# Load order and planner margins, a seven-product first layer for part of two chunks, and v casts and q features moved to other engines, in a fused linear attention and MLP kernel

## The chip, the cores and the metric

The kernel runs on one core of one Trainium2 chip. The metric is device time of one execution in microseconds (us). The kernel before takes 297.5 us (median of 4 runs, 297.03 to 297.73). All the ratios below use runs that were labelled fast; a median is over all runs of a kernel. TensorE, VectorE, ScalarE, GpSimd and the queue of SyncE are called PE, DVE, ACT, POOL and SP in the profile's lines; PEld is PE's weight load, which overlaps its matmuls.

## The reference, cut to what matters

```python
# q, k, v: (batch 8, heads 8, seq 576, head_dim 64), float32
phi(x) = concat(relu(x) * cos(theta * pos), relu(x) * sin(theta * pos))   # 64 -> 128 features
kv  = phi(k)^T v ;  z = sum(phi(k))                  # per batch and head
x   = (phi(q) @ kv) / (phi(q) @ z + 1e-6)            # 4608 tokens x 512
h   = x @ w_in                                       # first layer, 512 -> 2048
out = (h * cos(h)) @ w_out                           # second layer, 2048 -> 512
```

The 4608 tokens are worked in 9 chunks of 512. Chunks 0 to 7 are the first 512 tokens of each of the 8 batches, roughly; chunk 8 collects the 64 left over of each.

## The kernel before: the parts that matter here

The kernel does not issue instructions in the order of the program text. It records steps (engine, cost, what they read and write) in a `Plan`; a small model of the engines and of two DMA rings then orders the steps of each engine. On the chip each engine takes its instructions strictly in that order. A step that the model thought ready, but that waits for a late DMA, holds up all that stands behind it on its engine.

```python
class Plan:
    SHARE, WAKE, LAND = {"HW": 0.42, "SW": 0.58}, {"HW": 1.1, "SW": 1.6}, 1.0   # the DMA model
    ...
    def run(self):            # up to 12 passes: forward with keys, backward for new keys
```

Loads of q, k and v go through SyncE; the weights through GpSimd. An order between the two is made by small GpSimd copies ("holds") which write one element of a tile after another load has landed:

```python
def hold_raw(nm):             # batch 1: first heads of k, q, v wait for the first quarter of w_out
    pl.add("POOL", 0.2, 0.3, 0, lambda: nc.gpsimd.tensor_copy(
        out=raw[nm][0:2, 0, 0, 0:1], in_=w_out_sb[0:2, 0, 0:1]),
        [("w_out", 0)], [((nm, 0), 0), ((nm, 0), 1)])

def attention(b):             # batches 2 to 7
    ...                       # loads of k, q, v
    for t in range(NT + 1):
        for g in range(2):    # cosine and sine half of the features
            prep(b, "k", t, g, "DVE" if g == 0 else "ACT", T + 1.2 * t)
    for t in range(NT + 1):
        cast_v(b, t, "DVE", T + 6 + 0.4 * t)            # v to float16
    kv(b, T + 8)
    for t in range(NT + 1):
        ...
        for g in range(2):
            prep(b, "q", t, g, "DVE" if g == 0 else "ACT", due)
    ...

def layer1(c):                # chunks 2 to 8: 16 tiles of 4 matmuls of 128x512
    for n in range(NJT):
        ...
        for cc in range(NCT):
            nc.tensor.matmul(M1[m], lhsT=w_in_sb[:, cc, j * P:(j + 1) * P], rhs=X[:, cc, :],
                             start=(cc == 0), stop=(cc == NCT - 1))
        gate(...)             # ACT: cos(h);  DVE: h * cos(h) -> gT
```

The second layer already uses seven products in place of eight (Strassen's scheme in Winograd's form) for all chunks but the first. In the profile's names, km, qm, vm are the raw loads, kp and qp the features, V the float16 v, qT the transposed q features, x and xT the attention's result and its transpose, gT the gated hidden layer, ch its cosine, S and T the sums of the seven products of the second layer, ost the output. M, TR and ATT are PSUM banks.

## Time and profile before

| stretch, us | what PE does | PE idle | VectorE busy | ScalarE busy |
|---|---|---|---|---|
| 20 to 40 | chunk 0, first layer | 1.6 | 13.6 of 20 | 14.1 |
| 40 to 62 | attention 1, chunk 0's second layer | 4.6 | 16.8 of 22 | 15.3 |
| 62 to 82 | chunk 1 | 0.35 | 18.9 of 20 | 18.8 |
| 82 to 228 | chunks 1 to 6, attention 2 to 7 | 1.3 | 135.8 of 146 | 95.5 |
| 228 to 275 | chunks 7 and 8 | 0 | 32.9 of 47 | 24.6 |

These are the lines of the windows view of the kernel before. For each stretch they give its length, then busy us and number of instructions of PE, its weight loads, VectorE, ScalarE and GpSimd, then the granted share of PE's clock, the DMA engines' busy share and GB/s:

```profile
20.00:40.00 20.00, 18.36 (x151) 14.86 (x149) 13.62 (x28) 14.14 (x23) 1.07 (x5) 0.86 1.06 259
40.00:62.00 22.00, 17.41 (x193) 11.52 (x191) 16.84 (x41) 15.34 (x26) 1.31 (x2) 1.00 0.94 251
62.00:82.00 20.00, 19.65 (x235) 16.23 (x233) 18.85 (x38) 18.75 (x33) 0.00 (x0) 1.00 1.05 254
82.00:228.00 146.00, 144.71 (x1306) 100.15 (x1305) 135.84 (x279) 95.51 (x152) 0.00 (x0) 1.00 0.85 195
228.00:275.00 47.00, 47.00 (x315) 30.65 (x314) 32.88 (x53) 24.57 (x37) 0.00 (x0) 1.00 0.10 38
```

From 62 us on PE is the bound. VectorE is close behind it in the middle: 135.84 of 146 us is 93%. Before 62 us PE waits for data. The timeline of SyncE's queue shows why (start us, us, what):

```profile
14.77 0.60 SPq L295 DMA_DIRECT2D vm<-in_v_dram  x1
15.48 0.60 SPq L298 DMA_DIRECT2D vm<-in_v_dram  x1
29.23 0.60 SPq L298 DMA_DIRECT2D km<-in_k_dram  x1
```

The hold covers only the first heads of v. The second half of batch 1's v is issued at 14.77 us, and k of batch 1, which is needed first, at 29.23. On ScalarE a cast of this early v then stands in front of other work, and near 53 us a feature of k of batch 2 stands in front of a qT copy on VectorE. In these timeline lines of ScalarE and VectorE the bracket tells how long the engine was idle before the line and what ended it:

```profile
24.41 0.73 ACT L329 ACTIVATE V<-vm 128x256 f16<-128x256 f32 x2 [3.17 <-DMA vm<-in_v_dram]
...
53.15 0.88 DVE L319 TENSOR_SCALAR kp<-km,CS 128x512 f16<-128x512 f32 x2 [1.98 <-DMA km<-in_k_dram]
53.95 0.68 DVE L378 COPY qT<-M 128x1024 f16<-128x1024 f16 x1
```

PE pays for it. These are its longest waits in 40 to 62 us (who waited for whom: us in total, times, longest):

```profile
PE M L444 <- DVE qT L378: 2.3, 1, 2.3
PE ATT L404 <- DVE qT L378: 0.8, 1, 0.8
PE M L444 <- DVE x L424: 0.7, 1, 0.7
```

In 82 to 228 us the waits view lists one wait of PE, for a copy on ScalarE:

```profile
PE M L613 <- ACT ost L624: 1.3, 2, 1.1
```

Last, the groups by shape in 82 to 228 us, for the durations of VectorE's work (busy us, mean ns of one; then its idle time before them):

```profile
L466 DVE TENSOR_TENSOR gT<-M,ch 128x512 f16<-128x512 f32 x82 | 54.5, 683 | 6.6 <-ACT ch L464 6.0
L595 DVE TENSOR_TENSOR S<-gT 128x1024 f16<-128x1024 f16 x23 | 15.4, 683 | 0.1
L332 DVE CAST V<-vm 128x512 f16<-128x512 f32 x25 | 9.1, 421 | 0.0
L319 DVE TENSOR_SCALAR kp<-km,CS 128x512 f16<-128x512 f32 x20 | 9.0, 476 | 0.0
```

### The profile page before, as it was taken

How to read it: one execution, taken by the hardware profiler on the slowest of the kernel's cores; microseconds unless marked ns; L12 is line 12 of the kernel's file. 1: busy time of each engine (PE TensorE's matmuls, PEld its weight loads, DVE VectorE, ACT ScalarE, POOL GpSimd, SP SyncE). 2: the span in 40 equal slices, each digit the busy share in tenths (PEclk: the TensorE clock that was granted, in tenths of full speed). 3: DMA queues.
4: the chain of work that ended last, by engine and by line, in shares of the span. 5: the costliest groups of instructions: out<-in, count | busy, mean ns of one | idle time of the engine just before them, and what ended most of it. 6: DMA issues, size and time to landing. Idle time of an engine off the chain costs nothing.

```text
span 295.5 us, 6280 instructions
## 1 busy us (share of the span) xinstructions
PE 276.6 (94%) x2460; PEld 194.4 (66%) x2460; DVE 239.3 (81%) x486; ACT 183.6 (62%) x293; POOL 8.9 (3%) x20
## 2 busy tenths in 40 slices
PE   6768998699999999999999999999999999999994
PEld 2446866268977677666766766676668566666783
DVE  2975786798999899988998999999879858665741
ACT  2945895698987756767386849575544554645320
POOL 1520020000000000000000000000000000000000
PEclk9977999999999999999999999999999999999999
DMA  6999979999956999999999939971925100300304
GB/s 214 322 228 213 289 189 257 310 337 191 273 162 157 182 234 250 230 210 297 215 233 298 265 101 241 231 188 46 143 59 170 41 0 2 142 2 1 123 21 142
DMA packets 77565, 53.27 MB, mean 180 GB/s; under 512 B 46048, under 2 KB 75232, under 8 KB 77536
## 3 DMA queue, kind: packets, MB, share of 16 engines
q1 hardware_dynamic: 72592, 48.12, 63.9%
q0 software_dynamic: 4224, 4.19, 8.7%
q10 hardware_dynamic: 720, 0.57, 0.6%
q8 instruction: 19, 0.31, 0.4%
q14 instruction: 10, 0.08, 0.1%
HBM read 36.74 MB, written 9.44 MB: 156 GB/s over the span
## 4 chain that ended last, share of the span: by engine, by line
PE 67%; DMA 15%; DVE 9%; ACT 5%; issue 2%; SPq 0%; ACTq 0%; DVEq 0%
PE M L613 28%; PE M L509 27%; DMA vm<-in_v_dram 7%; PE M L491 6%; DMA qm<-in_q_dram 6%; DVE gT L466 3%; DMA km<-in_k_dram 3%; PE ATT L404 2%; PE ATT L343 2%; ACT ch L464 2%; DVE x L424 1%; PE M L553 1%; ACT kp L316 1%; ACT qp L316 1%; DVE V L332 1%
## 5 line engine op out<-in xcount | busy, mean ns | idle before, releaser
L464 ACT ACTIVATE ch<-M,PIH 128x512 f32<-128x512 f32 x144 | 97.9, 686 | 60.4 <-PE M L509 57.0
L466 DVE TENSOR_TENSOR gT<-M,ch 128x512 f16<-128x512 f32 x144 | 96.8, 685 | 25.8 <-ACT ch L464 24.9
L509 PE MATMUL M<-xT,w_in_sb 128*128 128x512 f16 x384 | 93.8, 379 | 0.0
L613 PEld LDWEIGHTS <-gT 128*128 128x128 f16 x640 | 62.4, 98 | 18.4 <-issue 1.7
L509 PEld LDWEIGHTS <-w_in_sb 128*128 128x128 f16 x448 | 42.1, 98 | 35.0
L613 PE MATMUL M<-w_out_sb,gT 128*128 128x256 f16 x384 | 46.8, 273 | 1.3 <-ACT ost L624 1.3
L491 PE MATMUL M<-xT,w_in_sb 128*128 128x256 f16 x256 | 31.8, 282 | 1.6 <-ACT xT L448 1.6
L613 PE MATMUL M<-T,S 128*128 128x256 f16 x256 | 32.5, 273 | 0.0
L613 PE MATMUL M<-T,gT 128*128 128x256 f16 x256 | 32.2, 273 | 0.0
L613 PEld LDWEIGHTS <-S 128*128 128x128 f16 x256 | 25.1, 98 | 8.0
L491 PEld LDWEIGHTS <-w_in_sb 128*128 128x128 f16 x256 | 25.5, 101 | 5.9 <-issue 2.1
L316 ACT ACTIVATE qp<-qm,CS 128x512 f16<-128x512 f32 x38 | 25.3, 713 | 6.5 <-DMA qm<-in_q_dram 6.5
L316 ACT ACTIVATE kp<-km,CS 128x512 f16<-128x512 f32 x39 | 26.4, 713 | 1.4 <-DMA km<-in_k_dram 1.4
L424 DVE TENSOR_TENSOR x<-ATT,rec 128x512 f16<-128x512 f32 x33 | 22.8, 691 | 1.1
L319 DVE TENSOR_SCALAR qp<-qm,CS 128x512 f16<-128x512 f32 x42 | 18.7, 484 | 5.7 <-DMA qm<-in_q_dram 5.7
L595 DVE TENSOR_TENSOR S<-gT 128x1024 f16<-128x1024 f16 x32 | 21.6, 685 | 0.2
L319 DVE TENSOR_SCALAR kp<-km,CS 128x512 f16<-128x512 f32 x41 | 18.3, 487 | 2.4 <-DMA km<-in_k_dram 2.4
L404 PEld LDWEIGHTS <-qT 128*128 128x128 f16 x320 | 14.7, 98 | 6.3 <-issue 2.7
L404 PE MATMUL ATT<-kvz,qT 128*128 128x65 f16 x296 | 14.8, 194 | 1.6 <-DVE qT L378 0.8
L509 PE MATMUL M<-xR,w_in_sb 128*128 128x512 f16 x64 | 16.1, 379 | 0.0
L332 DVE CAST V<-vm 128x512 f16<-128x512 f32 (+1 forms) x42 | 13.7, 382 | 2.9 <-DMA vm<-in_v_dram 2.9
L343 PEld LDWEIGHTS <-kp 128*128 128x128 f16 x320 | 10.9, 97 | 2.8 <-ACT V L329 1.1
(66 smaller groups left out, 180.2 us busy)
## 6 DMA issues: line engine op xcount, KB each, us to landing
out_dram<-ost SPq DMA_DIRECT2D x33, 256.0 KB, 3.0
qm<-in_q_dram SPq DMA_DIRECT2D x8, 640.0 KB, 6.4
km<-in_k_dram SPq DMA_DIRECT2D x8, 640.0 KB, 5.9
qm<-in_q_dram SPq DMA_DIRECT2D x8, 512.0 KB, 7.0
km<-in_k_dram SPq DMA_DIRECT2D x8, 512.0 KB, 6.7
vm<-in_v_dram SPq DMA_DIRECT2D x6, 640.0 KB, 5.5
vm<-in_v_dram SPq DMA_DIRECT2D x6, 512.0 KB, 5.5
w_in_sb<-in_moe_w_in_dram POOLq DMA_DIRECT2D x4, 512.0 KB, 10.1
```

Of the source, the lines that this page charges most:

```text
L316: act(0.12 + 0.5 * f, due, lambda: nc.scalar.activation(out=out_, in_=in_, func=AF.Relu, scale=sc), rd, wr)
L319: dve(0.09 + 0.33 * f, due, lambda: nc.vector.tensor_scalar(out=out_, in0=in_, scalar1=0.0, scalar2=sc, op0=ALU.max, op1=ALU.mult), rd, wr)
L332: dve(0.09 + 0.33 * f, due, lambda: nc.vector.tensor_copy(out=out_, in_=in_), rd, wr)
L343: nc.tensor.matmul(bank[hb][:, hh * D1:(hh + 1) * D1], lhsT=kp[:, t, h].rearrange("p g d -> p (g d)"), rhs=V1[:, t, h, :], start=(t == 0), ...
L404: nc.tensor.matmul(bank[hb][:, hh * D1:(hh + 1) * D1], lhsT=a[:, h, :], rhs=z[:, h, :], start=(i == 0), stop=(i == len(parts) - 1))
L424: nc.vector.tensor_tensor(out=split(x16[n][:, hs, :], k), in0=A[:, :, :, 0:D], in1=split(rec[n][:, hs], k).unsqueeze(3).broadcast_to((P, k ...
L464: act(0.59, due, lambda: nc.scalar.activation(out=ch[c], in_=bank, func=AF.Sin, bias=PIH, scale=1.0), [key, "PIH"], [("ch", c)])
L466: dve(0.61, due, lambda: nc.vector.tensor_tensor(out=dst, in0=bank if len(dst.shape) == 2 else bank.rearrange("p (j s) -> p j s", j=dst.sh ...
L491: nc.tensor.matmul(M1[m][:, jj * 2 * P:(jj + 1) * 2 * P], lhsT=w_in_sb[:, cc, j * P:(j + 1) * P], rhs=X[:, cc, ts], start=(cc == 0), stop= ...
L509: nc.tensor.matmul(M1[m], lhsT=w_in_sb[:, cc, j * P:(j + 1) * P], rhs=X[:, cc, :], start=(cc == 0), stop=(cc == NCT - 1))
L595: dve(0.07 + 1.07 / NG, due, lambda: nc.vector.tensor_tensor(out=out_[:, sl], in0=a[:, sl], in1=b[:, sl], op=op), rd, wr)
L613: nc.tensor.matmul(M2[bank][:, tt * MH:(tt + 1) * MH], lhsT=a[:, j, tt * P:(tt + 1) * P], rhs=b[:, j, :], start=(first and tt == 0 and j = ...
```

## The change

There are three parts.

- **Loads.** All of v is held, the holds wait for the third quarter of w_in in place of the first of w_out, the loads of the first two batches keep a fixed order, and the planner's DMA model gets new rates and lands each later load 1 us later.
- **Seven.** The first layer of chunk 7 (three groups of four) and of chunk 8 (two groups) uses seven products of half size in place of eight. This needs sums of w_in, built in the memory of kp and qp after batch 7, differences of x, and adds of the products.
- **Moves.** The v casts of batches 2 to 7 go from VectorE to GpSimd; the half of their q features that VectorE made goes to ScalarE.

```diff
-    SHARE, WAKE, LAND = {"HW": 0.42, "SW": 0.58}, {"HW": 1.1, "SW": 1.6}, 1.0
+    SHARE, WAKE, LAND = {"HW": 0.40, "SW": 0.56}, {"HW": 1.1, "SW": 1.3}, 1.0
+    BUSY, MARGIN = 2.2, 1.0
...
-                        done[n] = now + self.LAND
+                        done[n] = now + self.LAND + (self.MARGIN if now > 13.0 else 0.0)
...                                        # "lane": a fixed order for the first two batches' loads
+    GATE1 = (w_in_sb[0:2, 0, Dff // 2 + 1:Dff // 2 + 2], [("w_in", 2)])
...
     def hold_raw(nm):
-        pl.add("POOL", 0.2, 0.3, 0, lambda: nc.gpsimd.tensor_copy(
-            out=raw[nm][0:2, 0, 0, 0:1], in_=w_out_sb[0:2, 0, 0:1]),
-            [("w_out", 0)], [((nm, 0), 0), ((nm, 0), 1)])
+        for h in (0, HB) if nm == ORDER1[2] else (0,):
+            pl.add("POOL", 0.2, 0.3, 0, lambda h=h: nc.gpsimd.tensor_copy(
+                out=raw[nm][0:2, h, 0, 0:1], in_=GATE1[0]),
+                GATE1[1], [((nm, h), 0), ((nm, h), 1)])
...
+    FAST1 = {B - 1: 3, B: 2}
...                                        # w_in_sums(): 8 sums of 128x1024 on VectorE
+        def tt(n, a, b, op, rd, wr):
+            for f in range(2):
+                fs = slice(f * JH * P // 2, (f + 1) * JH * P // 2)
+                dve(0.61, due, lambda fs=fs: nc.vector.tensor_tensor(
+                    out=WS[n][:, :, fs], in0=a[:, :, fs], in1=b[:, :, fs], op=op),
+                    wk + [(x, f) for x in rd], wr + [("WS%d" % n, f)])
...                                        # layer1_fast(): 7 products of 4 matmuls of 128x256 a group
+            d = product(A, -11, b11, xk, True, False)
+            copy(Y, A, zk[0], d)
+            d = product(Bk, -12, b21, xk, True, True)
+            plus(Y, Bk, zk[0], d)
+            out(Y, zk[0], 0, 0, d)
...                                        # five more products
         for t in range(NT + 1):
-            cast_v(b, t, "DVE", T + 6 + 0.4 * t)
+            cast_v(b, t, "POOL", T + 6 + 0.4 * t)
...
             for g in range(2):
-                prep(b, "q", t, g, "DVE" if g == 0 else "ACT", due)
+                prep(b, "q", t, g, "ACT", due)
```

More of the change, by code (lines that the diff above doesn't have):

```diff
@@ L36, in __init__, with add @@
         self.steps = []
-        self.wr, self.rd = {}, {}
-    def add(self, eng, occ, lat, due, fn, rd=(), wr=(), dma=None):
+        self.wr, self.rd, self.lanes = {}, {}, {}
+    def add(self, eng, occ, lat, due, fn, rd=(), wr=(), dma=None, lane=None):
         n = len(self.steps)
+        prev = self.lanes.get(lane)
+        if lane is not None:
+            self.lanes[lane] = n
         deps = set()
@@ L55, in add @@
         self.steps.append(dict(eng=eng, occ=occ, lat=lat, due=due, fn=fn,
-                               deps=deps, dma=dma, n=n))
+                               deps=deps, dma=dma, n=n, prev=prev))
         return n
@@ L85, in forward @@
                 users[d].append(s["n"])
+        follow = {s["prev"]: s["n"] for s in st if s["prev"] is not None}
+        left = [k + (s["prev"] is not None) for k, s in zip(left, st)]
         avail, start, done = [0.0] * len(st), [0.0] * len(st), [0.0] * len(st)
@@ L123, in forward @@
                         n = rings[r].pop(0)[2]
-                        done[n] = now + self.LAND
+                        if r == "SW" and not rings["SW"]:
+                            for x in rings["HW"]:
+                                x[0] = min(x[0], max(now, x[3]))
+                        done[n] = now + self.LAND + (self.MARGIN if now > 13.0 else 0.0)
                         release(n)
@@ L134, in forward @@
             free[e] = t + s["occ"]
+            if n in follow:
+                u = follow[n]
+                avail[u] = max(avail[u], t)
+                left[u] -= 1
+                if not left[u]:
+                    ready[st[u]["eng"]].append(u)
             if s["dma"] is None:
@@ L140, in forward @@
                 r = "SW" if e == "POOL" else "HW"
-                rings[r].append([free[e] + self.WAKE[r], s["dma"][0] / s["dma"][1], n])
+                wake = free[e] + self.WAKE[r]
+                late = wake + (self.BUSY if r == "HW" and rings["SW"] and not rings["HW"] else 0.0)
+                rings[r].append([late, s["dma"][0] / s["dma"][1], n, wake])
         return start, done
@@ L149, in backward @@
                 left[d] += 1
+            if s["prev"] is not None:
+                left[s["prev"]] += 1
         limit = [end - done[n] + start[n] for n in range(len(st))]
@@ L171, in backward @@
                 limit[d] = min(limit[d], late[n] - self.link(d, n) - (done[d] - start[d]))
+                left[d] -= 1
+                if not left[d]:
+                    ready[st[d]["eng"]].append(d)
+            d = st[n]["prev"]
+            if d is not None:
+                limit[d] = min(limit[d], late[n] - 0.01)
                 left[d] -= 1
@@ L265 @@
     Q_PE, X_PE = (), range(1, 3)
+    ORDER0, ORDER1, HOLDW = "qkv", "kqv", 1
+    GATE1 = (w_in_sb[0:2, 0, Dff // 2 + 1:Dff // 2 + 2], [("w_in", 2)])
     src = {"k": k, "v": v, "q": q}
@@ L299, in load @@
             nb = len(part) * R * D * 4 / 1e3
-            pl.add("SP", 0.65, 0, due, go4, (), [(x, 1 - n) for x in part], dma=(nb * NT, 355.0))
-            pl.add("SP", 0.65, 0, due, go5, (), [(x, n) for x in part], dma=(nb * (NT + 1), 355.0))
+            pl.add("SP", 0.65, 0, due, go4, (), [(x, 1 - n) for x in part], dma=(nb * NT, 355.0),
+                   lane="first" if b < 2 else None)
+            pl.add("SP", 0.65, 0, due, go5, (), [(x, n) for x in part], dma=(nb * (NT + 1), 355.0),
+                   lane="first" if b < 2 else None)
     def hk(nm, hs=range(H)):
@@ L330, in cast_v @@
                 out=out_, in_=in_, func=AF.Copy), rd, wr)
+        elif eng == "POOL":
+            pl.add("POOL", 0.9, 1.0, due, lambda: nc.gpsimd.tensor_copy(
+                out=out_, in_=in_), rd, wr)
         else:
@@ L500, in layer1 @@
             return
-        for n in range(NJT):
-            j = n // 2 + (n % 2) * JH if c < B else n
+        if c in FAST1:
+            layer1_fast(c, X, xk)
+        for n in range(4 * FAST1.get(c, 0), NJT):
+            j = n // 2 + (n % 2) * JH if c < B or c in FAST1 else n
             m = m1n[0] % NM1
@@ L512, in layer1, with flat, wsum @@
             gate(M1[m], ("M1", m), G[:, j, :], [("g", c % 2, j, t) for t in range(NT)], due + 1.5)
+    FAST1 = {B - 1: 3, B: 2}
+    CH2 = NCT // 2
+    def flat(t, dt=F16):
+        v = t.rearrange("p a b c -> p (a b c)") if len(t.shape) == 4 else t.rearrange(
+            "p a b c d -> p (a b c d)")
+        return v if dt == F32 else v.bitcast(F16)
+    kf, qf = flat(kp), flat(qp)
+    n2 = CH2 * JH * P
+    def wsum(ap, n):
+        return ap[:, n * n2:(n + 1) * n2].rearrange("p (c f) -> p c f", c=CH2)
@@ new lines, with w_in_sums @@
+    WS = {2: wsum(kf, 0), 3: wsum(kf, 1), 1: wsum(qf, 0), 4: wsum(qf, 1)}
+    Z3 = [[flat(raw[nm], F32)[:, i * SM:(i + 1) * SM] for i in range(3)] for nm in "kqv"]
+    XSS = [[flat(raw[nm])[:, 6 * SM + i * SM:6 * SM + (i + 1) * SM].rearrange(
+        "p (c s) -> p c s", c=CH2) for i in range(4)] for nm in "kq"]
+    def w_in_sums():
+        lo, hi = slice(0, JH * P), slice(JH * P, Dff)
+        W = w_in_sb
+        a11, a12, a21, a22 = W[:, 0:CH2, lo], W[:, CH2:, lo], W[:, 0:CH2, hi], W[:, CH2:, hi]
+        gone = {nm: [(nm + "p", t, g, h) for t in range(NT + 1) for g in range(2) for h in range(H)]
+                for nm in "kq"}
+        wk = [("w_in", g) for g in range(4)]
+        due = start[B - 1] - 6
+        def tt(n, a, b, op, rd, wr):
[4 more added lines that the diff above has]
+                    wk + [(x, f) for x in rd], wr + [("WS%d" % n, f)])
+        tt(3, a11, a21, ALU.subtract, [], gone["k"])
+        tt(1, a21, a22, ALU.add, [], gone["q"])
+        tt(2, WS[1], a11, ALU.subtract, ["WS1"], [])
+        tt(4, a12, WS[2], ALU.subtract, ["WS2"], [])
@@ new lines, with layer1_fast, tt, lhs @@
+    g1n = [0]
+    def layer1_fast(c, X, xk):
+        G = gT[c % 2]
+        tl, th = slice(0, TH), slice(TH, SM)
+        b11, b12 = X[:, 0:CH2, tl], X[:, 0:CH2, th]
+        b21, b22 = X[:, CH2:, tl], X[:, CH2:, th]
+        w0, ww = start[c], width[c]
+        XS = XSS[c % 2]
+        def tt(n, a, b, rd, wr=()):
+            dve(0.33, w0 - 1 + 0.3 * n, lambda: nc.vector.tensor_tensor(
+                out=XS[n], in0=a, in1=b, op=ALU.subtract), xk + rd, [("XS", c % 2, n)] + list(wr))
+        tt(0, b12, b11, [], (hk("k") + hk("q") + hk("v") + ["AL"]) if c == B - 1 else ())
+        tt(2, b22, b12, ["AL"])
+        tt(1, b22, XS[0], [("XS", c % 2, 0)])
+        tt(3, b21, XS[1], [("XS", c % 2, 1)])
+        ng = JH // 2
+        for g in range(FAST1[c]):
+            A, Bk = BANKS[g1n[0] % 4], BANKS[(g1n[0] + 1) % 4]
+            st_ = (g1n[0] // 2) % 3
+            g1n[0] += 2
+            Y, U, Z = Z3[st_]
+            zk = [("Z3", st_, i) for i in range(3)]
+            j0 = 2 * g
+            order = iter(range(1, 8))
+            def lhs(n):
+                if n > 0:
+                    return (lambda cc, j, j0=j0: WS[n][:, cc, (j0 + j) * P:(j0 + j + 1) * P],
+                            [("WS%d" % n, g // 2)])
+                hj, hc = {-11: (0, 0), -12: (0, 1), -22: (1, 1)}[n]
+                return (lambda cc, j, j0=j0: w_in_sb[:, hc * CH2 + cc, (hj * JH + j0 + j) * P:
+                                              (hj * JH + j0 + j + 1) * P],
+                        [("w_in", q_) for q_ in range(4)])
+            def product(bank, n, b, rd, first, last):
+                due = w0 + (g + next(order) / 7) / ng * ww
+                a, ak = lhs(n)
+                def mm():
+                    for j in range(2):
+                        for cc in range(CH2):
+                            nc.tensor.matmul(
+                                bank[0][:, j * TH:(j + 1) * TH], lhsT=a(cc, j), rhs=b[:, cc, :],
+                                start=(first and j == 0 and cc == 0),
+                                stop=(last and j == 1 and cc == CH2 - 1), skip_group_check=True)
+                pe(2 * CH2, MMH, due, mm, rd + ak, [bank[1]])
+                return due
+            def copy(dst, bank, key, due):
+                act(0.5, due + 0.3, lambda: nc.scalar.activation(out=dst, in_=bank[0], func=AF.Copy),
+                    [bank[1], "AL"], [key])
+            def plus(dst, bank, key, due):
+                dve(0.61, due + 0.3, lambda: nc.vector.tensor_tensor(
+                    out=dst, in0=bank[0], in1=dst, op=ALU.add), [bank[1], key], [key])
+            def out(src_, key, hj, ht, due):
+                js = slice(hj * JH + j0, hj * JH + j0 + 2)
+                gate(src_, key, G[:, js, ht * TH:(ht + 1) * TH],
+                     [("g", c % 2, j, t) for j in range(js.start, js.stop)
+                      for t in (2 * ht, 2 * ht + 1)], due + 1.5)
+            d = product(A, -11, b11, xk, True, False)
[3 more added lines that the diff above has]
+            out(Y, zk[0], 0, 0, d)
+            d = product(A, 2, XS[1], [("XS", c % 2, 1)], False, False)
+            copy(U, A, zk[1], d)
+            d = product(Bk, 1, XS[0], [("XS", c % 2, 0)], True, False)
+            copy(Z, Bk, zk[2], d)
+            d = product(A, 3, XS[2], [("XS", c % 2, 2)], False, False)
+            plus(Z, A, zk[2], d)
+            out(Z, zk[2], 1, 1, d)
+            d = product(Bk, 4, b22, xk, False, True)
+            plus(U, Bk, zk[1], d)
+            out(U, zk[1], 0, 1, d)
+            d = product(A, -22, XS[3], [("XS", c % 2, 3)], False, True)
+            out(A[0], A[1], 1, 0, d)
@@ L686, in hold @@
                 out=w_in_sb[0:1, 0, :].rearrange("p (g f) -> p g f", g=4)[:, :, 0],
-                in_=raw["k"][0:1, 0, 0, 0:1].broadcast_to((1, 4)))
-        pl.add("POOL", 0.4, 0.5, 0, hold, hk("k"), [("w_in", g) for g in range(4)])
+                in_=raw[ORDER0[1]][0:1, 0, 0, 0:1].broadcast_to((1, 4)))
+        pl.add("POOL", 0.4, 0.5, 0, hold, hk(ORDER0[1]), [("w_in", g) for g in range(4)])
         for g in range(4):
@@ L707, in hold_raw, with rest_of_w_out @@
     def hold_raw(nm):
-        pl.add("POOL", 0.2, 0.3, 0, lambda: nc.gpsimd.tensor_copy(
-            out=raw[nm][0:2, 0, 0, 0:1], in_=w_out_sb[0:2, 0, 0:1]),
-            [("w_out", 0)], [((nm, 0), 0), ((nm, 0), 1)])
-    def rest_of_w_out():
+        for h in (0, HB) if nm == ORDER1[2] else (0,):
+            pl.add("POOL", 0.2, 0.3, 0, lambda h=h: nc.gpsimd.tensor_copy(
+                out=raw[nm][0:2, h, 0, 0:1], in_=GATE1[0]),
+                GATE1[1], [((nm, h), 0), ((nm, h), 1)])
+    def rest_of_w_out(nm):
         def hold():
@@ L715, in hold @@
                 out=w_out_sb[0:1, JH:, 0].rearrange("p (g j) -> p g j", g=2)[:, :, 0],
-                in_=raw["q"][0:1, 0, 0, 0:1].broadcast_to((1, 2)))
-        pl.add("POOL", 0.2, 0.3, 0, hold, hk("q"), [("w_out", g) for g in (2, 3)])
+                in_=raw[nm][0:1, 0, 0, 0:1].broadcast_to((1, 2)))
+        pl.add("POOL", 0.2, 0.3, 0, hold, hk(nm), [("w_out", g) for g in (2, 3)])
         w_out_load(2, 4)
@@ L724, in first_attention @@
         warm(14, 6.5)
-        for nm, hs in (("q", (slice(0, H),)), ("k", (slice(0, H),)), ("v", HALVES)):
-            load(0, nm, 0, hs)
+        for nm in ORDER0:
+            load(0, nm, 0, HALVES if nm == ORDER0[2] else (slice(0, H),))
         weights()
@@ L745, in second_attention @@
         T = start[1] - 30
-        for nm, hs in (("k", (slice(0, H),)), ("q", (slice(0, H),)), ("v", HALVES)):
+        for nm in ORDER1:
             hold_raw(nm)
-            load(1, nm, T, hs)
-            if nm == "q":
-                rest_of_w_out()
+            load(1, nm, T, HALVES if nm == ORDER1[2] else (slice(0, H),))
+            if nm == ORDER1[HOLDW]:
+                rest_of_w_out(nm)
         for t in range(NT + 1):
@@ L808 @@
             attention(c)
+        if c == B - 1:
+            w_in_sums()
         layer2(c - 1)
```

## The prediction

> **What bounds the kernel now.** From 62 to 291.1 us TensorE. The windows view gives PE busy 19.65 of 20 us (62:82), 144.7 of 146 (82:228) and 63.1 of 63.1 (228:291.1); the chain of waits there is almost only first- and second-layer matmuls at full rate: 0.863 us per 4 of 128x512 and 0.872 us per 8 of 128x256, so 216 and 109 ns each. The other PE idle lies before 20 us (6.6), in 20:62 (6.2) and at the tail (4.4).
>
> The 20:62 idle is a load-order problem. The timeline of the DMA queue shows the second half of batch 1's v issued at 14.8 us, while k1, q1 and the rest of v1 wait for a GpSimd hold until 29.2. ScalarE, in order, stands 3.2 us before a cast of that early v, and PE waits 0.95 us for an xT copy behind it. Later VectorE stands 2.0 us for k2 (53.2), and PE 2.3 us behind it for a qT copy. The first layer of chunk 1 starts only at 60.2. The DMA share is about 0.9 to 1.2 up to 62 us: only the order can improve.
>
> **The change.**
> 1. Loads: all of v1 is held; k1, q1, v1 start when the third w_in quarter has landed (about 21 us, my estimate), not the first w_out quarter (29). The planner assumes DMAs 1 us later, so fewer in-order stalls. x1 comes some 7 us earlier and chunk 1's first layer fills idle time: 3.5 to 4 of the 6.2 us.
> 2. Seven products: a group costs 28 x 0.109 = 3.05 us in place of 16 x 0.2157 = 3.45; five groups save 2.0 us, all on the critical chain. Added on VectorE: 8 weight sums (0.69 each), 8 input differences (0.36), 15 adds (0.69), 19 us; on ScalarE 15 copies (0.60), 9 us. In 228:291 VectorE is busy 41 of 63 us, ScalarE 29: it fits.
> 3. 30 v casts (0.42 each, 12 us) leave VectorE for GpSimd; 30 q features (0.475, 14 us) go to ScalarE (0.71, 21 us). VectorE, at 9.3 tenths in 82:228, falls to about 7.5; ScalarE rises from 6.5 to about 8. That gives only the 1.3 us of PE idle there, of which I take 0.8. A GpSimd cast should take 0.6 to 1 us (its 128x512 memset took 0.52). The Trainium skill, "SBUF — State Buffer", section "SBUF: two separate sides", says that GpSimd and a VectorE instruction in a two-port mode or with two SBUF inputs exclude each other for a whole instruction. This trace cannot show it; I expect some longer VectorE instructions.
>
> Sum: 3.7 + 2.0 + 0.8, less 0.3 of new waits: 6.2 us.
>
> **Predicted: 291.2 us, range 287.8 to 294.8. Faster by over 2%: 0.52; within 2%: 0.46; slower: 0.02.**
>
> **What would show it.** PE idle in 20:62 falls from 6.2 to about 2.5, k1 issued near 21 us; PE busy total falls by about 2 us; 144 gates as before, 140 fast matmuls; VectorE busy about 232 us, ScalarE about 214; PE without gaps from about 60 us on, up to 0.5 us.
>
> **What would make it wrong.** Earlier loads take bandwidth from w_in and w_out, and PE waits for weights. DMA share is near 1 in 108:189, so a PE that is 4 us ahead may wait for x of chunks 3 to 5 and give the gain back. GpSimd casts far over 1 us, or lock waits on VectorE. The interleaved last chunk may open a gap before its second layer.

## The result, and the profile after

The changed kernel takes 293.35 us (median of 4 runs, 292.24 to 293.87); the ratio to the kernel before is 0.9857, with a 95% interval of 0.9823 to 0.9891. All ratios here are the mean time of one kernel's fast runs over the mean of the other's fast runs in the same rounds, so they are not quite the ratio of the medians quoted. Two other chips gave 0.9887 (0.9857 to 0.9917) and 0.9854 (0.9820 to 0.9887) for the same kernel. The output was correct in every run reported here.

So the gain is 3.4 to 4.3 us, not 6.2. It lies inside the predicted range; the central value was 2 us too low.

The windows view after:

```profile
20.00:40.00 20.00, 17.94 (x160) 14.74 (x161) 15.11 (x30) 15.90 (x25) 3.77 (x7) 1.00 1.15 281
40.00:62.00 22.00, 18.73 (x212) 12.62 (x211) 18.56 (x37) 16.80 (x30) 6.27 (x5) 1.00 0.98 281
62.00:82.00 20.00, 20.00 (x253) 17.40 (x251) 18.04 (x38) 19.58 (x35) 3.30 (x5) 1.00 1.07 272
82.00:228.00 146.00, 144.66 (x1290) 99.66 (x1287) 127.69 (x234) 109.53 (x178) 15.77 (x20) 1.00 0.82 191
228.00:275.00 47.00, 47.00 (x386) 37.52 (x385) 44.11 (x77) 32.48 (x54) 0.00 (x0) 1.00 0.12 40
```

Read against the lines of before, two things are odd. PE's idle time in 20 to 62 us fell only from 6.2 to 5.3 us. And in 82 to 228 us PE still loses 1.3 us, though VectorE now has 8 us less to do there. The timeline of SyncE's queue shows that the new order is what was meant; k of batch 1 starts 11 us earlier and both halves of v follow q:

```profile
18.40 0.60 SPq L326 DMA_DIRECT2D km<-in_k_dram  x1
...
25.57 0.60 SPq L326 DMA_DIRECT2D qm<-in_q_dram  x1
...
28.83 1.86 SPq L326 DMA_DIRECT2D vm<-in_v_dram  x1
```

The stall near 50 us is still there, on ScalarE now, with the xT copies behind it; PE's waits in 40 to 62 us follow:

```profile
50.41 2.56 ACT L346 ACTIVATE kp<-km,CS 128x512 f16<-128x512 f32 x4 [3.06 <-DMA km<-in_k_dram]
52.87 1.05 ACT L481 ACTIVATE xT<-M 128x512 f16<-128x512 f16 x2
```

```profile
PE ATT L437 <- DVE x L457: 2.0, 2, 1.2
PE M L477 <- ACT xT L481: 1.1, 1, 1.1
```

In 82 to 228 us the wait for ScalarE's ost copy is gone, PE's only wait is a new one (waits view), and the groups by shape show what became of VectorE's instructions:

```profile
PE M L544 <- DVE gT L499: 1.2, 3, 0.6
```

```profile
L499 DVE TENSOR_TENSOR gT<-M,ch 128x512 f16<-128x512 f32 x81 | 54.2, 682 | 11.4 <-ACT ch L497 10.9
L362 POOL CAST V<-vm 128x512 f16<-128x512 f32 x20 | 15.8, 837 | 86.0 <-PE ATT L376 86.0
L751 DVE TENSOR_TENSOR S<-gT 128x1024 f16<-128x1024 f16 x21 | 15.5, 746 | 0.2
L349 DVE TENSOR_SCALAR kp<-km,CS 128x512 f16<-128x512 f32 x20 | 11.7, 631 | 0.0
```

VectorE's k features went from 476 to 631 ns and its sums S from 683 to 746 ns, while the gates, which read PSUM, stayed at 682. The timelines of GpSimd and of VectorE around the PE wait show it instruction by instruction:

```profile
168.39 3.88 POOL L362 CAST V<-vm 128x512 f16<-128x512 f32 x5 [26.09 <-PE ATT L376]
```

```profile
168.43 1.11 DVE L751 TENSOR_TENSOR S<-gT 128x1024 f16<-128x1024 f16 x1
169.47 2.33 DVE L349 TENSOR_SCALAR kp<-km,CS 128x512 f16<-128x512 f32 x3
```

These lines are merged. In the single records of this trace, the three k features start at 169.47, 170.22 and 170.97 us and last 0.83 us each, and the casts beside them start at 169.96, 170.71 and 171.46 us and last 0.81: each engine starts one every 0.75 us, in turn. Of the 20 k features in 82 to 228 us, the 9 that overlap a cast took 0.825 to 0.831 us, and the 11 others 0.466 to 0.473. This is what the Trainium skill, "SBUF — State Buffer", section "SBUF: two separate sides", describes as an exclusive lock, held for the whole instruction, between GpSimd and a VectorE instruction in a two-port mode or with two SBUF inputs. The trace agrees, also in that the gate, with one PSUM input, is untouched: the 7 gates of this trace that overlap a cast took 0.67 to 0.69 us.

### Where the time went: PE's lag

"Busy" hides one thing. A matmul at half clock counts as busy (in the half-clock piece of the kernel before, 256-column matmuls start 0.213 us apart, and 0.109 outside it). To see lost time whatever its kind, I worked out from each trace when PE had started a given amount of matmul work, counted at the full-speed durations that the traces show (215.7 ns for 512 columns, 109 for 256, 57 for a 128-column transpose, 31 for 65; warm-up matmuls left out). The lag is that time minus the work. All PE work is 263.37 us before and 261.37 after: the seven products save 2.00 us of work by this count.

```
lag of PE in us, when this much work has been started (us)      half-clock pieces
                    7     25     35     60    140    180    260    begun before 60 us, us
before           19.5   19.5   25.0   25.6   27.3   27.3   27.5      6.8
loads alone      18.1   19.4   21.1   21.7   22.8   22.7   23.0      3.4
moves alone      20.4   21.9   30.5   30.5   32.8   32.7   33.0     17.1
seven alone      20.0   21.4   24.9   25.5   26.7   26.7   28.6     10.2
loads + seven    17.3   17.9   20.4   21.3   22.6   22.5   24.3      0.0
loads + moves    19.5   19.8   22.2   23.3   24.0   25.3   25.5      6.8
all (after)      17.7   17.9   22.2   22.3   23.0   24.3   24.5      3.4
```

The last column is the time at half the clock by the trace's clock records, in pieces that began before 60 us. It comes in pieces of 3.41 us or multiples, at other places in each execution, and so the lag at 7 and 25 us of work varies by 1 to 3 us between profiles of one kernel (after: 17.7, 18.5 and 20.1 at 7 us in three profiles). Differences in the early columns are not to be read to a microsecond from one profile. The growth from 60 to 260 us of work has no half-clock time in it and repeats: 2.2, 2.2 and 2.0 us for the changed kernel.

### The profile page after: what moved, and what is told of

Its sections match the earlier page's. It is cut to its first block, busy times and chain, and to the rows that moved or that the text cites. A ratio compares the mean times of both kernels' runs of the same rounds, so it can differ in the third digit from the quotient of the medians.

```text
span 290.5 us, 6468 instructions
## 1 busy us (share of the span) xinstructions
PE 274.0 (94%) x2520; PEld 200.2 (69%) x2520; DVE 241.4 (83%) x457; ACT 206.6 (71%) x338; POOL 34.2 (12%) x51
## 4 chain that ended last, share of the span: by engine, by line
PE 75%; DVE 10%; DMA 7%; ACT 5%; issue 2%; DVEq 0%; ACTq 0%
PE M L769 30%; PE M L544 24%; PE M L524 7%; DMA km<-in_k_dram 5%; PE M L632 4%; PE ATT L437 3%; DVE gT L499 2%; DMA qm<-in_q_dram 2%; PE M L709 2%; DVE kp L349 2%; ACT ch L497 2%; DVE x L457 1%; ACT kp L346 1%; PE ATT L376 1%; DVE gT L796 1%
## 5 line engine op out<-in xcount | busy, mean ns | idle before, releaser
L497 ACT ACTIVATE ch<-M,PIH 128x512 f32<-128x512 f32 x129 | 87.6, 685 | 36.5 <-PE M L544 30.7
L499 DVE TENSOR_TENSOR gT<-M,ch 128x512 f16<-128x512 f32 x129 | 86.5, 683 | 17.6 <-ACT ch L497 17.0
L544 PE MATMUL M<-xT,w_in_sb 128*128 128x512 f16 x336 | 83.1, 379 | 1.3 <-DVE gT L499 1.2
L544 PEld LDWEIGHTS <-w_in_sb 128*128 128x128 f16 x368 | 34.8, 98 | 30.8 <-issue 2.4
L346 ACT ACTIVATE qp<-qm,CS 128x512 f16<-128x512 f32 x68 | 45.9, 714 | 5.6 <-DMA qm<-in_q_dram 5.6
L362 POOL CAST V<-vm 128x512 f16<-128x512 f32 x30 | 25.3, 893 | 109.1 <-PE ATT L376 86.0
L524 PE MATMUL M<-xT,w_in_sb 128*128 128x256 f16 x256 | 30.2, 272 | 0.9 <-ACT xT L481 0.7
L524 PEld LDWEIGHTS <-w_in_sb 128*128 128x128 f16 x256 | 24.6, 98 | 4.4 <-issue 1.2
L457 DVE TENSOR_TENSOR x<-ATT,rec 128x512 f16<-128x512 f32 x33 | 22.8, 691 | 1.1
L349 DVE TENSOR_SCALAR kp<-km,CS 128x512 f16<-128x512 f32 x41 | 21.4, 572 | 0.7 <-DMA km<-in_k_dram 0.6
L751 DVE TENSOR_TENSOR gT<-gT 128x1024 f16<-128x1024 f16 x16 | 11.4, 712 | 0.2
L709 PE MATMUL M<-w_out_sb,gT 128*128 128x512 f16 x48 | 11.2, 379 | 0.2 <-DVE gT L499 0.2
```

The source lines that it names most:

```text
L346: act(0.12 + 0.5 * f, due, lambda: nc.scalar.activation(out=out_, in_=in_, func=AF.Relu, scale=sc), rd, wr)
L349: dve(0.09 + 0.33 * f, due, lambda: nc.vector.tensor_scalar(out=out_, in0=in_, scalar1=0.0, scalar2=sc, op0=ALU.max, op1=ALU.mult), rd, wr)
L362: pl.add("POOL", 0.9, 1.0, due, lambda: nc.gpsimd.tensor_copy(out=out_, in_=in_), rd, wr)
L457: nc.vector.tensor_tensor(out=split(x16[n][:, hs, :], k), in0=A[:, :, :, 0:D], in1=split(rec[n][:, hs], k).unsqueeze(3).broadcast_to((P, k ...
L497: act(0.59, due, lambda: nc.scalar.activation(out=ch[c], in_=bank, func=AF.Sin, bias=PIH, scale=1.0), [key, "PIH"], [("ch", c)])
L499: dve(0.61, due, lambda: nc.vector.tensor_tensor(out=dst, in0=bank if len(dst.shape) == 2 else bank.rearrange("p (j s) -> p j s", j=dst.sh ...
```

## The experiments

Twelve runs were made (ten edited kernels, and the changed kernel twice), on three chips, each with five rounds against the kernel before. Undoing all three parts of the changed program gives the program of the kernel before again, instruction for instruction (built and compared, not run), so the parts are complete.

### The three parts alone, and the changed kernel again

loads_only is the kernel before with the loads part; relative to the changed kernel:

```diff
-    FAST1 = {B - 1: 3, B: 2}
+    FAST1 = {}
-        if c == B - 1:
-            w_in_sums()
-            cast_v(b, t, "POOL", T + 6 + 0.4 * t)
+            cast_v(b, t, "DVE", T + 6 + 0.4 * t)
-                prep(b, "q", t, g, "ACT", due)
+                prep(b, "q", t, g, "DVE" if g == 0 else "ACT", due)
```

> The kernel before with the load order, the holds and the planner's margins alone (plain first layer, v casts and q features where they were). Theory A, the prediction's: this part is worth 3.5 to 4 us, so a ratio of 0.986 to 0.989. Theory B: most of the drop in lag before 62 us in the two first profiles (1.75 us by 26 us) came from where the half-clock slot fell (18.7 to 25.6 us before, 8.5 to 12.0 after), not from the order, so this part is worth about 1 us, a ratio of 0.995 to 0.999. The profile's clock row and the lag of PE behind its own work at 7, 35 and 60 us of work tell them apart; k2 should still be waited for near 50 us.

Measured: 292.65 us median, ratio 0.9855 (0.9822 to 0.9889). The loads alone bring 4.3 us, as much as the whole change. Theory B is refuted, in its size: the order is worth far more than 1 us. Part of the path may still be the clock: over its six runs the mean granted clock was 0.992, and 0.982 over the 33 runs of the kernel before. Within kernels, 0.01 less of clock goes with about 1.2 us more of span (71 runs, correlation 0.62), so about 1 us of the 4.3 may come with fewer half-clock pieces (in the two profiles, 0.9 of the 4.5 us between their lags is the surplus of half-clock matmuls over their full-speed durations). Whether these are cause or consequence of the stalls no run here settles.

moves_only undoes the loads part and the seven products, and keeps the moves. The undone loads part is in both this and the next kernel:

```diff
+    SHARE, WAKE, LAND = {"HW": 0.42, "SW": 0.58}, {"HW": 1.1, "SW": 1.6}, 1.0
+    BUSY, MARGIN = 0.0, 0.0
+        lane = prev = None
-        for h in (0, HB) if nm == ORDER1[2] else (0,):
+        for h in (0,):
+    GATE1 = (w_out_sb[0:2, 0, 0:1], [("w_out", 0)])
```

> The kernel before with the 30 v casts on GpSimd and the 30 q features on ScalarE alone. Theory A, the prediction's: 0.8 us, ratio about 0.997, since only 1.3 us of PE idle lay in the middle. Theory B: GpSimd casts lock VectorE out, its k features stretch from 0.48 to 0.78 us while a cast runs, and the 1.3 us of idle is replaced by as much: ratio 1.000 within 0.002.

Measured: 301.57 us median, ratio 1.0141 (1.0096 to 1.0185). Both theories fail: the moves alone cost 4.2 us. The lag table has the largest growth between 25 and 35 us of work (8.6 us, against 5.5 in the kernel before). There the timeline of ScalarE shows a longer form of the stall known from before, and the waits view shows PE behind it (40 to 62 us):

```profile
55.06 0.72 ACT L346 ACTIVATE kp<-km,CS 128x512 f16<-128x512 f32 x1 [4.60 <-DMA km<-in_k_dram]
55.69 1.00 ACT L409 ACTIVATE qT<-M 128x1024 f16<-128x1024 f16 x1
```

```profile
PE M L477 <- ACT qT L409: 2.6, 1, 2.6
PE M L477 <- ACT xT L481: 1.9, 1, 1.9
```

The lock is not to blame for these waits: the first GpSimd cast of that run starts at 58.6 us. With other costs the planner made another order, in which a qT copy for chunk 1 stands behind a k feature of batch 2. But this stall is the smaller part of that profile's loss. It also has two half-clock pieces, 10.2 us from 20.2 us on and 6.8 us from 57.8 us on. The surplus of the matmuls that start in such pieces over their full-speed durations is 3.7 us up to 25 us of work and 2.3 us between 25 and 35, against 2.1 and 0 in the kernel before. So about 4 of the 5.5 us by which this profile is behind at 260 us of work are half-clock matmuls, and under 2 are waits. That the moves alone cost time is measured; even the run with the highest mean clock (0.985) took 298.88 us. Why the half-clock pieces were longer in this profile, and how much of the 4.2 us comes with them, stays open.

seven_only undoes the loads and the moves and keeps the seven products.

> The kernel before with the seven-product first layer alone, VectorE not relieved. Theory A, the prediction's: additive, 2.0 us, ratio 0.993. Theory B: VectorE has no room for the weight sums and adds without the moves, PE waits for it around chunks 6 to 8, and little or nothing is left: ratio 0.998 to 1.002, with PE waits on VectorE after 200 us.

Measured: 296.50 us median, ratio 0.9988 (0.9957 to 1.0019): 0.4 us. The additive 2.0 us (0.993) is excluded. The lag grows by 3.1 us between 60 and 260 us of work, where the kernel before has 1.9: about 1.2 of the 2.0 us saved are given back, as theory B had it. The place is as late as expected (26.7 at 180 us of work, 28.6 at 260).

after_again is the changed kernel itself, unedited:

> The changed kernel itself, again, on the chip and in the rounds of the three others: ratio 0.984 to 0.988 if the first measurement holds. If the parts are additive, the three other gains sum to this one. The profile shows whether the half-clock slot falls in the same place again (8.5 to 12.0 us) or moves from run to run.

Measured: 293.48 us median, ratio 0.9887 (0.9857 to 0.9917), just above the expected range. The parts do not add: 4.3 - 4.2 + 0.4 is 0.5 us, and the whole brings 3.4 in these rounds. The half-clock pieces fell elsewhere, as said above.

### Two parts together

no_moves has the loads and the seven products.

> The changed kernel without the moves, that is the new loads and the seven products: v casts and half of the q features on VectorE. Theory B: VectorE has no room, so the seven products give back what they save: ratio 0.985 to 0.989, no better than the new loads alone (0.9855). Theory A, additive: 2 us better than the loads alone, 0.979.

Measured: 292.08 us median, ratio 0.9836 (0.9812 to 0.9861). This is 0.6 us better than the loads alone, inside the noise of both, and worse than the additive 0.979, which is outside its interval. It lies just below theory B's range (0.985 to 0.989), which its interval overlaps. Its PE waits in 82 to 228 us are these:

```profile
PE M L769 <- ACT ost L780: 1.0, 1, 1.0
PE ATT L437 <- DVE x L457: 0.7, 1, 0.7
```

The second one comes with the seven products. VectorE's timeline at that point shows five weight sums (out of w_in_sb, into kp and qp) in front of the normalisation of x, for which PE waits:

```profile
217.16 0.68 DVE L580 TENSOR_TENSOR qp<-w_in_sb 128x1024 f16<-128x1024 f16 x1
217.75 1.28 DVE L580 TENSOR_TENSOR kp<-qp,w_in_sb 128x1024 f16<-128x1024 f16 x2
218.96 1.28 DVE L580 TENSOR_TENSOR qp<-w_in_sb,kp 128x1024 f16<-128x1024 f16 x2
220.16 0.16 DVE L453 TENSOR_SCALAR den<-ATT 128x8 f32<-128x8 f32 x1
220.35 0.20 DVE L455 RECIPROCAL rec<-den 128x8 f32<-128x8 f32 x1
220.59 0.69 DVE L457 TENSOR_TENSOR x<-ATT,rec 128x512 f16<-128x512 f32 x1
```

The matmuls whose result den reads ended at 218.07 us; PE's next ones of that kind start at 221.33, after 0.66 us of idle time that the end of x closes. Between 195 and 200 us of work, where this falls, the lag grows by 1.1 us, and between 205 and 210, in the first fast products, by 0.4. The loads alone lose nothing at either place; seven_only loses 1.1 and 0.6.

no_seven has the loads and the moves.

> The changed kernel without the seven products, that is the new loads and the moves. If the moves cost what the lag shows (about 1 us before 60 us, 1.2 us at 165 to 174), and the seven products still save their 2.0 us in the whole kernel, this is 2 us slower than the changed kernel: ratio 0.9945. If the seven products give nothing even with the moves, it equals the changed kernel: 0.988.

Measured: 295.05 us median, ratio 0.9945 (0.9926 to 0.9965), the value expected. Against the loads alone (0.9855) the moves cost 2.7 us; the intervals are apart. Some of it may again be clock (mean 0.987 over six runs against 0.992, about 0.7 us by the relation above). After 60 us of work, where no half-clock time is, the lag grows by 2.2 us against 1.3. Against the changed kernel (0.9857, 0.9887, 0.9854, mean 0.9866) the seven products are worth 2.3 us. So with the moves they give their full 2.0 us, and without them 0.4 to 0.6 us (each of these figures is good to about 1 us, by the intervals).

### The GpSimd casts

casts_on_dve is the changed kernel with the v casts back on VectorE:

```diff
-            cast_v(b, t, "POOL", T + 6 + 0.4 * t)
+            cast_v(b, t, "DVE", T + 6 + 0.4 * t)
```

> The changed kernel with the 30 v casts put back on VectorE; q features stay on ScalarE, loads and seven products stay. Lock theory: GpSimd casts cost PE about 1.2 us in 165 to 174 us because VectorE's k features (0.63 us each in 82 to 228 us, 0.476 before) and sums (0.75, 0.68 before) wait for them; without them these durations return to 0.48 and 0.68, the 1.2 us PE wait on gT goes, and the ratio falls by about 0.003 to 0.984. Rival, room: VectorE needs the 12 us, and without the casts' removal PE waits for VectorE elsewhere: ratio 0.990 or more.

Measured: 292.29 us median, ratio 0.9851 (0.9823 to 0.9880). The groups by shape of this run, 82 to 228 us:

```profile
L751 DVE TENSOR_TENSOR S<-gT 128x1024 f16<-128x1024 f16 x22 | 14.7, 684 | 0.2
L349 DVE TENSOR_SCALAR kp<-km,CS 128x512 f16<-128x512 f32 x20 | 8.7, 478 | 0.0
```

Both durations are back at their old values, PE has no wait there at all (its busy time is 146.00 of 146 us), and the lag grows by 0.2 us between 60 and 260 us of work, against 2.0 to 2.2. That is as the lock theory has it, and "VectorE has no room" is wrong once the q features are on ScalarE. A fall of the time is not shown: 0.9851 lies 0.0015 under the mean of the changed kernel's three ratios, inside the noise, and its profile had two half-clock pieces near the start and a lag of 24.3 at 60 us. This version is also planned anew, so the order of its steps differs; the next experiment keeps the order.

casts_twice does every GpSimd cast twice; the instructions of PE, VectorE and ScalarE stand in the same order as in the changed kernel, in both traces:

```diff
-            pl.add("POOL", 0.9, 1.0, due, lambda: nc.gpsimd.tensor_copy(
-                out=out_, in_=in_), rd, wr)
+            pl.add("POOL", 0.9, 1.0, due, lambda: [nc.gpsimd.tensor_copy(
+                out=out_, in_=in_) for _ in range(2)], rd, wr)
```

> The changed kernel with every GpSimd cast done twice; all other engines' instructions stand in the same order. Lock theory: GpSimd's time in casts doubles from about 25 us, the stretch of VectorE's k features and sums about doubles (k features on VectorE to about 0.75 us on average), the PE waits on gT grow from 1.2 to 2.5 us or more, and the time rises by 1 to 3 us. Rival, room: GpSimd has 85% of its time free and nothing waits for it: no change beyond 0.3 us.

Measured: 297.51 us median, ratio 1.0024 (1.0001 to 1.0046), 4 to 5 us over the changed kernel, more than expected. A group line and the PE wait of 82 to 228 us:

```profile
L349 DVE TENSOR_SCALAR kp<-km,CS 128x512 f16<-128x512 f32 x20 | 14.3, 764 | 0.0
```

```profile
PE M L544 <- DVE gT L499: 3.2, 5, 1.2
```

The k features stretch to 764 ns, the wait grows from 1.2 to 3.2 us, the growth of the lag from 2.2 to 4.3 us. With the last experiment this shows the cause of that wait from both sides: without casts no wait, with twice the casts nearly three times the wait. (That growth is 2.1 us of the added time. Another 1 to 2 us arise between 35 and 60 us of work, where the casts of batches 2 and 3 run: the lag goes from 21.9 to 23.8 there, and by 0.0 to 0.7 in three profiles of the changed kernel.)

### The loads part, split

holds_only has the new holds and the fixed order, but the planner's old rates and no margin; planner_only the reverse. Both are without seven products and moves.

```diff
 holds_only (against loads_only)
-    SHARE, WAKE, LAND = {"HW": 0.40, "SW": 0.56}, {"HW": 1.1, "SW": 1.3}, 1.0
-    BUSY, MARGIN = 2.2, 1.0
+    SHARE, WAKE, LAND = {"HW": 0.42, "SW": 0.58}, {"HW": 1.1, "SW": 1.6}, 1.0
+    BUSY, MARGIN = 0.0, 0.0
 planner_only (against loads_only)
+        lane = prev = None
-        for h in (0, HB) if nm == ORDER1[2] else (0,):
+        for h in (0,):
-    GATE1 = (w_in_sb[0:2, 0, Dff // 2 + 1:Dff // 2 + 2], [("w_in", 2)])
+    GATE1 = (w_out_sb[0:2, 0, 0:1], [("w_out", 0)])
```

> Of the loads part only the order: the second batch's loads held until the third w_in quarter has landed, both halves of v held, a fixed order of the first two batches; the planner's old rates and no margin. If the order carries the gain: ratio 0.985 to 0.988, as with the whole loads part (0.9855). If the margins carry it: 0.995 or more, with PE waits on ScalarE or VectorE that stand before k2 near 50 us.

Measured: 294.64 us median, ratio 0.9902 (0.9864 to 0.9940).

> Of the loads part only the planner's rates and its 1 us margins; the holds as before. If the order carries the gain: 0.996 to 1.002. If the margins do: 0.988 or less.

Measured: 295.92 us median, ratio 0.9906 (0.9853 to 0.9960). These two varied more than the others (292.4 to 296.8 and 292.2 to 297.6), and the slowest of them were left out of the ratios; with all six runs planner_only comes nearer to 0.995. Neither expectation is met cleanly, and the shares are not settled. The traces still say what each does. With the holds PE has no idle time in 40 to 62 us (busy 22.00 of 22 us), and the lag stays at 21.1 from 25 to 35 us of work; then it grows to 25.1 at 260, first by a wait of 1.1 us for a qT transfer at 72.7 us. With the planner's margins alone the old stall stays, the lag goes from 18.8 to 26.0 between 25 and 35 (about 1.5 us of that in a half-clock piece that begins at 56.6 us), and then grows by only 0.3 us up to 260. So in these profiles, one of each kernel, the order removes the early stall. With order and margins together (loads_only) the lag stands at the same 21.1 at 35 us of work and ends at 23.0, so the margins go with about 2 us less of loss later.

### A version meant to beat both

q4_casts_dve keeps the loads and the seven products, has the casts on VectorE, and gives ScalarE all q features only from batch 4 on:

```diff
-            cast_v(b, t, "POOL", T + 6 + 0.4 * t)
+            cast_v(b, t, "DVE", T + 6 + 0.4 * t)
-                prep(b, "q", t, g, "ACT", due)
+                prep(b, "q", t, g, "DVE" if g == 0 and b < 4 else "ACT", due)
```

> A version meant to beat both: new loads, seven products, all v casts back on VectorE (no GpSimd lock), and the q features wholly on ScalarE only from batch 4 on; batches 2 and 3 split them as before, so that ScalarE's queue is free while x of chunk 1 waits in it. If the lock and the early ScalarE queue are what the moves cost, and ScalarE's share of the q features later is what gives VectorE room for the seven products, then the lag is about 21.7 at 60 us of work as with the loads alone, grows by less than 0.7 after that, and the ratio is 0.976 to 0.981. If the seven products need the casts gone too, PE waits on VectorE after 200 us and the ratio stays at 0.984 or above.

after_control is the changed kernel, unedited, in the same rounds:

> The changed kernel in the rounds of the three others, so that the version meant to beat it is compared on one chip: ratio 0.984 to 0.990.

Measured: q4_casts_dve 291.14 us median, ratio 0.9810 (0.9766 to 0.9854); the changed kernel in the same rounds 292.78 us median, 0.9854 (0.9820 to 0.9887). The version is 5.6 us faster than the kernel before. It is 1.3 us ahead of the changed kernel by means, but the intervals meet, so that step is likely and not shown. It fell short of what was expected in two points: the lag at 60 us of work was 22.3 and not 21.7, and it grew by 1.8 us between 60 and 260 us of work and not by under 0.7, over half of it in small PE waits in 82 to 228 us for a gate (0.5), for x (0.3) and for a PSUM copy (0.2).

## Why the prediction was right or wrong, point by point

- **The total.** Predicted 291.2 us with a range of 287.8 to 294.8; measured 293.35. The range held it, the direction was right, and the gain was two thirds of what was forecast. The likelier class, faster by over 2% (0.52), did not come: all three ratios of the changed kernel are within 2%. That the total fell inside the range is in part luck. Put on one after the other, the loads brought 4.3 us (forecast 3.7), the moves -2.7 (forecast +0.8) and the seven products 2.3 (forecast 2.0); one wrong sign was covered by a range of 7 us and by a surplus elsewhere.
- **"From 62 to 291.1 us TensorE".** Right: the lag of the kernel before grows by only 1.9 us after 60 us of work.
- **"3.5 to 4 of the 6.2 us" from the loads.** Right in size: alone they bring 4.3 us (3.3 to 5.3 by the interval). The sign that was named for it holds less well: with all three parts PE idle in 20 to 62 us went to 5.3 us (4.4 and 4.1 in the two other profiles) and not to 2.5, and with the loads alone to 3.3. k of batch 1 was issued at 18.4 us (forecast 21). The last part of chunk 1's x began at 52.9 us in place of 59.0, 6.1 us earlier (forecast 7), but its first layer started at 57.4 us in place of 60.2. The idle column of one profile does not measure this part alone, because half-clock matmuls count as busy: the window 20 to 40 us had a mean clock of 0.86 before and 1.00 after. The margin did not remove the k2 stall: ScalarE stood 3.06 us, as VectorE had stood 1.98.
- **"five groups save 2.0 us, all on the critical chain".** Right as work (263.37 to 261.37 us) and right with the moves in place (2.3 us). As an independent term it was wrong: alone it is worth 0.4 us. The prediction checked VectorE's room only where the fast products run, in 228 to 291 us. The sums of w_in have to be made before that, in 206 to 220 us in the run with the loads and the seven products; VectorE is at 93% up to 228 us, and PE waits for x behind five sums.
- **"That gives only the 1.3 us of PE idle there, of which I take 0.8" for the moves.** This is the step that failed, in its sign. Added to the loads they cost 2.7 us (0.9945 against 0.9855). The lock was foreseen, with its page, but was costed at nothing: "I expect some longer VectorE instructions". It was not a few: in 82 to 228 us the 20 k features of VectorE went from 476 to 631 ns, because the five casts of a batch come back to back, just when k features do. The saving itself did come: the kernel before and the loads alone lose 1.0 to 1.3 us of lag between 110 and 115 us of work, where PE waits for the ost copy, and the runs with the moves lose nothing there. But the changed kernel and no_seven lose 0.5 us between 90 and 95 and 1.3 us between 145 and 150 us of work, where casts run, and casts_on_dve loses nothing at either place: PE's wait of 1.2 us for gates is the same size as the wait that went away. The rest of the cost lies before 60 us; at equal half-clock time (3.4 us) the lag at 60 us is 22.3 with the moves and 21.7 without, and in moves_only the reordered ScalarE queue is seen at work, beside half-clock matmuls that cost more. How the early share divides between queue and clock stays open.
- **The sum of terms.** The moves make room for the seven products, and cost about what these then save: together they bring nothing on top of the loads (the three ratios of the whole, mean 0.9866, against 0.9855 for the loads alone). The prediction added the parts; on an engine that is nearly full they are not independent.
- **The signs named.** 140 fast matmuls (512-column ones fell from 536 to 456, 24 of them for warm-up in both, 256-column ones rose from 1152 to 1292), 144 gates: right. VectorE's busy time of 232 us: it was 241.4, in part through the lock. ScalarE 214: it was 206.6. "PE without gaps from about 60 us on, up to 0.5 us": 1.3 us in 82 to 228 us, 1.2 of it the waits for gates of the run with the lock.
- **"a PE that is 4 us ahead may wait for x of chunks 3 to 5".** Did not happen: loads alone keep their lead (lag 21.7 at 60, 22.8 at 140).

## What to carry to other kernels

Before adding the gains of several moves, ask which engine each one loads in the stretch where it runs, sums made ahead of time included; on an engine at 93% a saving elsewhere is first paid for there. A cast that goes to an idle GpSimd is not free if VectorE works on SBUF in the same stretch: compare the durations of VectorE's instructions by shape, and look for two engines that go in turn. Measure each part alone, and compare kernels by PE's lag behind its own work, since half-clock matmuls look busy.

## What the Trainium skill lacked or had wrong

- "SBUF — State Buffer", section "SBUF: two separate sides": right about the lock, and silent on its size in such a case. Here five back-to-back GpSimd casts of 128x512 from float32 to float16 and VectorE's k features of the same shape went in turn, one of each every 0.75 us, and a k feature that overlaps a cast took 0.83 us against 0.47 for one that does not; the mean over 82 to 228 us rose to 0.631, and to 0.764 with twice the casts. A gate with one PSUM input kept its 0.68 us.
- "GPSIMD Engine Reference", section "4.1 Engine selection": one-input work is called roughly line-rate on GpSimd. The float32 to float16 cast of 128x512 took 0.84 us on GpSimd on average in 82 to 228 us (0.81 in turn with k features), 0.62 us where only VectorE instructions with a PSUM input ran beside it (4 casts of the changed kernel's trace, 0.617 to 0.624), and 0.42 us on VectorE. GpSimd's spans in a profile are rough.
- "TensorE: Matmul & The Clock Gate", section "Part 1: The HAM clock gate (the "warmup" mystery)": it names a window of 3413 ns and a half-rate clock that activity releases, and says the place varies from run to run. The clock records agree (pieces of 3.41 us and multiples, at 0.5, other places in each execution). It advises that the ramp is under 1% of a typical span. That is said of the ramp; here further pieces begin as late as 57.8 us, those begun before 60 us make 0 to 17 us in all and cost 0 to 6 us by the surplus of their matmuls, and 0.01 of mean clock went with 1.2 us of span within a kernel, which is the size of the differences to be told apart.
- No page has the lag used here, which puts waits and half-clock matmuls into one number and shows where in the kernel they arise (a total for the half-clock part alone the skill does have). The lag separated 2 us of given-back time from 3 us of scatter at the start.
